# Linear attention in a fused attention and mixture-of-experts kernel: key-value sums with the features as weights, in two column halves

## The chip, the cores and the metric

One core of a Trainium2 chip runs the whole program. The metric is device time in microseconds (us), the median of several executions. TensorE (PE) multiplies, its weight loads are listed as PEld; VectorE (DVE), ScalarE (ACT) and GpSimd (POOL) do the rest, and SyncE (SP) issues most DMAs. Matrices are float32; the program issues one matmul instruction where the trace shows two.

## The reference

```python
def _attn_ref(q, k, v, w_phi):            # (4, 8, 576, 64) each
    def phi(x):
        proj = np.einsum('bhsd,df->bhsf', x, w_phi)              # f = 128
        proj = proj - np.max(np.abs(proj), axis=-1, keepdims=True)
        return np.concatenate([np.exp(proj), np.exp(-proj)], axis=-1)
    q_p, k_p = phi(q), phi(k)
    kv = np.einsum('bhsf,bhsd->bhfd', k_p, v)
    z = np.sum(k_p, axis=2)
    num = np.einsum('bhsf,bhfd->bhsd', q_p, kv)
    den = np.einsum('bhsf,bhf->bhs', q_p, z)[..., None] + 1e-06
    return num / den
```

The result, 2304 tokens of 512, goes through a first mixture of 8 experts (one expert per token, only for tokens whose product with `w_skip` is positive) and a second one in which every token passes every expert. The gate of the first needs, per token, its product with `w_gate` (8 columns) and `w_skip` (1 column): 9 columns more for each head.

## The kernel before

The attention comes first. Two batches and two heads make a unit; there are 8 units of 9 tiles of 128 rows each, for keys and for queries. The loop over `g` in `attention` has 37 passes, and this text counts them from 0. A pass projects two pairs of tiles (`pp`, line 130), centres them on DVE (`m` and `t`, lines 137 and 139, one after the other), takes both exponentials on ScalarE (`f`, lines 146 and 147), and meanwhile works on the features of the pass before: query features are turned on TensorE (`ptq`, line 200, copied to `fq`), key features go into the key-value sums (`kv`, line 160), and numerator, denominator and gate columns come out of `num` (`po`, line 210), which `finish` divides on DVE (`rd`, `x`, `lall`). TensorE, DVE and ScalarE run in the order in which the code is written; POOL's and SP's order is set by a scheduler.

In `kv_mm` the values are the weights (128 rows, 64 columns and a column of ones) and the 256 features stream. The sums stand in PSUM with the 65 value columns as partitions. When a batch of a unit is complete (16 times in all, called blocks here), ScalarE copies the sums out (`kvt`, line 172); in the next pass `augment` multiplies them by `aug`, a table with an identity and the head's gate columns, which turns them and appends 9 columns (`pa`, line 187), and ScalarE copies that to `kvf` (line 194). `pt`, `ptq`, `pa` and `po` share four PSUM banks in turn.

The finished rows go to DRAM three times for the first two batches (`xd0`, `xd`, `x2d`), and twice for the others. After the first half, `Router.route` computes each token's place, and nine scatters on POOL write token numbers into `idx`. From pass 26 on the generator `moe1` fetches the first expert's weights (`fetch`, `fetch2`), and from pass 28 it splits one eighth of them into high and low parts at the end of each pass (`w1h` on ScalarE, `w1l` on DVE). The first expert slot starts when the attention ends.

Of the kernel before, what the change touches and what calls it, by code (L numbers as in the profile page):

```python
# [7 lines left out]
F32 = mybir.dt.float32  # L8
# [4 lines left out]
AF = mybir.ActivationFunctionType  # L13
# [5 lines left out]
P = 128  # L19
B, H, S, DH, FH = 4, 8, 576, 64, 128  # L20
# [18 lines left out]
def attention(tc, nc, cp, q, k, v, w_phi, w_gate, w_skip, lgs, routed, stepped, early, last_steps):  # L39
# [3 lines left out]
    with ExitStack() as ctx:  # L43
        c1 = ctx.enter_context(tc.tile_pool(name="c1", bufs=1))
        wk = ctx.enter_context(tc.tile_pool(name="wk", bufs=2))
        ps = ctx.enter_context(tc.tile_pool(name="psA", bufs=1, space=PSUM))
# [8 lines left out]
            nc.vector.memset(tab, 0.0)  # L55
            nc.scalar.activation(tab, tab, AF.Exp)

        aug = c1.tile([65, H, P], F32, name="aug")

        def load_aug():  # L60
            nc.gpsimd.memset(aug, 0.0)
            nc.sync.dma_start(aug[0:64, :, 65:73], w_gate.rearrange("(h d) e -> d h e", d=DH))
            nc.sync.dma_start(aug[0:64, :, 73:74], w_skip.rearrange("(h d o) -> d h o", d=DH, o=1))
            nc.gpsimd.tensor_copy(aug[:, :, 0:65], ident[0:65, 0:65].unsqueeze(1).to_broadcast([65, H, 65]))

        lall = c1.tile([P, 672], F32, name="lall")[:, 0 : NJ * H * 9].rearrange("p (j h e) -> p j h e", j=NJ, h=H)

        def bank(shape, nm):
            return ps.tile(shape, F32, name=nm, tag="W", bufs=4)
# [80 lines left out]
        def kv_mm(f, i, w):  # L150
            u, j = divmod(w, NJ)
            vt = st["vt", u]
            bs = [b for b in range(2) if 4 * b <= j <= 4 + 4 * b]
            for b in bs:
                if j == 4 * b:
                    st["acc", b] = ps.tile([65, 2, 256], F32, name="kv", tag="K", bufs=2)
            for h in range(2):
                for b in bs:
                    pr = slice(0, P) if j != 4 else slice(64 * b, 64 * b + 64)
                    nc.tensor.matmul(  # L160
                        st["acc", b][:, h],
                        vt[pr, j, h, 0:65],
                        f[pr, i % 2, i // 2 * 2 + h].rearrange("p s f -> p (s f)"),
                        start=(j == 4 * b and h == 0),
                        stop=(j == 4 * b + 4 and h == 1),
                        skip_group_check=True,
                    )
            done = [(u, b) for b in bs if j == 4 * b + 4]
            for u, b in done:
                kvt = wk.tile([65, 2, 256], F32, name="kvt", tag="kvt")  # L170
                st["kvt", u, b] = kvt
                late.append(lambda kvt=kvt, acc=st["acc", b]: nc.scalar.activation(kvt, acc, AF.Copy))
            if j == NJ - 1:
                load("vt", u + 2)
            return done

        def augment(u, b):
            kvt = st.pop(("kvt", u, b))
            hp = units[u][1]
            if b == 0:  # L180
                st["kv", u] = wk.tile([P, 608], F32, name="kvf", tag="kvf")[:, 0:592].rearrange(
                    "p (b h s f) -> p b h s f", b=2, h=2, s=2
                )
            pa = bank([P, 2, 2, P], "pa")
            for h in range(2):
                for fb in range(2):
                    nc.tensor.matmul(
                        pa[:, h, fb],
                        kvt[:, h, fb * P : fb * P + P],
                        aug[:, 2 * hp + h],  # L190
                        start=True,
                        stop=True,
                    )
            nc.scalar.activation(st["kv", u][:, b], pa[:, :, :, 0:74], AF.Copy)

        def q_tr(f, i, fq, o):
            pt = bank([P, 4, P], "ptq")
# [59 lines left out]

        for nm, u in (("kt", 0), ("vt", 0), ("kt", 1), ("qt", 0)):
            load(nm, u)
        load_aug()  # L260
        for nm, u in (("vt", 1), ("qt", 1)):
            load(nm, u)
        for u in (2, 3):
# [10 lines left out]
        with tc.manual_schedule(engines={nc.tensor.engine, nc.vector.engine, nc.scalar.engine}):  # L274
            busy(9)
            th = transp(steps[0])
            busy(8)
            for g in range(len(steps) + 1):
                cur = steps[g] if g < len(steps) else []
                if cur:  # L280
                    if g:
                        t = center(proj(th))
                    else:
                        nth = transp(steps[1])
                        t = center(proj(th))
                        th = nth
                        busy(16)
                    if 0 < g < len(steps) - 1:
                        th = transp(steps[g + 1])
                    if g == 1:  # L290
                        busy(8)
                tl = {m: [(2 * i + r, w + r) for i, (nm, w) in enumerate(prev) if nm == m for r in range(2)] for m in "kq"}
                qs = tl["q"]
                fqs = []
                for o, (i, w) in enumerate(qs):
                    if o % 2 == 0:
                        fqs.append(wk.tile([P, 2, 4, P], F32, name="fq", tag="fq"))
                    q_tr(f, i, fqs[-1], o % 2)
                for ub in aug_todo:
                    augment(*ub)  # L300
                aug_todo = []
                f_ = expo(t) if cur else None
                for i, w in tl["k"]:
                    aug_todo += kv_mm(f, i, w)
                for c in late:
                    c()
                late.clear()
                if not cur:
                    last_steps(ps)
                for o, fq in enumerate(fqs):  # L310
                    ws_ = [w for _, w in qs[2 * o : 2 * o + 2]]
                    finish(ws_, num(ws_, fq))
                f, prev = f_, cur
                stepped()
                if cur:
                    early(g)
# [223 lines left out]
def moe1(tc, nc, c, rt, w1, w2, idx, xd, xd0, x2d, route, end):  # L540

    with ExitStack() as ctx:
# [7 lines left out]
        tabs = []  # L550
        xTs = [[early.tile([P, NKB, SLOT], F32R, name=nm) for nm in ("xTh0", "xTl0")]]

        def fetch(s):
            t, i = (first[s], 0) if s < 2 else (tabs[1], s - 2)
            e = nc.sync.value_load(t[0:1, 0, i : i + 1], min_val=0, max_val=E - 1)
            r = nc.sync.value_load(t[0:1, 1, i : i + 1], min_val=0, max_val=NIDX - SLOT)
            if s == 0:
                load_r1(e)
            src, n = (xd0, NTOK // 2) if s < 2 else (xd, NTOK)
            ix, xg = ixs[s % 3], xgs[s % 3]  # L560
            ins = nc.sync.dma_start(ix, idx[bass.ds(r, SLOT)].rearrange("(a p) o -> p a o", p=P))
            if s in (0, 2):
                for o in rt.scatters:
                    tc.add_manual_dep(
                        ins.ins,
                        o.ins.name,
                        mybir.DependencyInfo(mybir.DependencyClass.Sync, mybir.DependencyReason.DATA),
                        reason="the list is complete",
                    )
            nc.gpsimd.memset(xg, 0.0)  # L570
            for a in range(2):
                nc.gpsimd.indirect_dma_start(
                    out=xg[:, a],
                    out_offset=None,
                    in_=src[:, :],
                    in_offset=bass.IndirectOffsetOnAxis(ap=ix[:, a].bitcast(U32), axis=0),
                    bounds_check=n - 1,
                    oob_is_err=False,
                )
            if s:  # L580
                load_r1(e)
            return e

        def load_r1(e):
            for kb in range(NKB):
                nc.sync.dma_start(
                    r1[:, kb], w1[bass.ds(e, 1), kb * P : kb * P + P].rearrange("o p f -> p (o f)")
                )

        def fetch2(e):  # L590
            for f in range(0, NFB, 2):
                nc.sync.dma_start(
                    r2[:, f : f + 2],
                    w2[bass.ds(e, 1), f * P : f * P + 2 * P].rearrange("o (b p) d -> p (o b) d", p=P),
                )
# [5 lines left out]
        def split_w1(i):  # L601
            kb, h = divmod(i, 2)
            sl = slice(512 * h, 512 * h + 512)
            split_w(w1h[:, kb, sl], w1l[:, kb, sl], r1[:, kb, sl])
# [87 lines left out]
                    slot(s)  # L692
                    chain(s + 1)

        rt.scatter()
        es = rt.early_slots()
        first = [next(es)]
        fetch2(fetch(0))
        yield
        first.append(next(es))  # L700
        done, psA = 0, None
        while psA is None:
            psA = yield
            for i in range(done, min(8, done + 1) if psA is None else 8):
                split_w1(i)
                done += 1
        e1 = fetch(1)
# [452 lines left out]
def tile_kernel(  # L1160
# [25 lines left out]
    late, gates = [], []  # L1186

    def stepped():
        rt.scatter(3)
        if gates:  # L1190
            gates.pop(0)()

# [74 lines left out]
```

## Time and profile before

| | |
|---|---|
| median of 3 runs | 2007.0 us (2003.72 to 2011.33) |
| the profiled execution | 2020.51 us, of it 2018.7 us span |
| attention, from the start to the first matmul of the first slot | 239.8 us |
| TensorE busy over the span | 1982.6 us (98%) |
| mean granted clock over the span | 0.992 |

A busy TensorE isn't TensorE at its peak, since the ends of matmuls are modelled; so the text goes by the distance from one group's start to the next one's. DMA share is the mean busy share of 16 DMA engines; over 1 means that packets overlap, which is a full queue.

### The profile page before, as it was taken

The page shows a single profiled execution, that of the slowest core. Times are in us where ns is not written, and L with a number is a line of the kernel's source. Part 1 is how long each engine was busy: PE and PEld are TensorE (multiplying, and loading weights), DVE is VectorE, ACT ScalarE, POOL GpSimd, SP SyncE. Part 2 cuts the span into 40 slices and gives each one's busy share as a digit, 9 for nine tenths or more (in the row PEclk, how much of TensorE's full clock was granted, in tenths as well). Part 3 has the DMA queues.
Part 4 walks back from the last instruction along what each step waited for, and adds up shares of the span by engine and source line. Part 5 has one row for each costly group of instructions (what it writes and reads, how often), then busy time and mean ns, then how long its engine had stood idle before and what let it go on. Part 6 is the DMA issues. An engine that isn't in the chain of part 4 may idle for free.

```text
span 2018.7 us, 30705 instructions
## 1 busy us (share of the span) xinstructions
PE 1982.6 (98%) x11752; PEld 1748.9 (87%) x11752; DVE 1250.4 (62%) x2134; ACT 893.9 (44%) x1706; POOL 339.2 (17%) x281
## 2 busy tenths in 40 slices
PE   9999999989999999999999999999999999999999
PEld 7877899986788988989888999899988888898997
DVE  4555777765676666666646666665664666556663
ACT  5665745545443433434344343343434434334441
POOL 1002032211112121121012212112101121212210
PEclk9998999999999999999999999999999999999999
DMA  7996776645312122131121212213112121221211
GB/s 167 105 133 143 124 235 221 216 154 169 107 36 84 49 77 73 53 115 55 45 83 59 84 42 84 74 53 115 52 48 89 53 84 42 84 74 53 84 53 42
DMA packets 163355, 187.40 MB, mean 93 GB/s; under 512 B 38334, under 2 KB 116926, under 8 KB 163196
## 3 DMA queue, kind: packets, MB, share of 16 engines
q1 hardware_dynamic: 159580, 178.17, 32.1%
q0 software_dynamic: 3456, 7.09, 1.1%
q8 instruction: 95, 1.56, 0.3%
q14 instruction: 64, 0.52, 0.1%
q10 hardware_dynamic: 160, 0.07, 0.0%
HBM read 163.70 MB, written 23.96 MB: 93 GB/s over the span
## 4 chain that ended last, share of the span: by engine, by line
PE 71%; DMA 3%; DVE 2%; ACT 1%; SPq 1%; issue 0%; ACTq 0%
PE py L1016 36%; PE pb L980 14%; PE pd L980 9%; PE pa L980 9%; DMA r<-in_moe_w_dram 3%; PE pg L857 1%; PE warm L730 1%; SPq L777 1%; DVE wcl L807 1%; ACT w2h L966 0%; PE pt L849 0%; DVE hl L1001 0%; DMA xr<-x2d 0%; DVE c L1068 0%; ACT v L988 0%
## 5 line engine op out<-in xcount | busy, mean ns | idle before, releaser
L1016 PE MATMUL py<-w2l,hh 128*128 128x512 f32 x1152 | 452.3, 393 | 0.0
L1016 PE MATMUL py<-w2h,hh 128*128 128x512 f32 x1152 | 451.6, 392 | 0.0
L1016 PE MATMUL py<-w2h,hl 128*128 128x512 f32 x1152 | 451.1, 392 | 0.0
L971 DVE TENSOR_TENSOR w2l<-r,w2h 128x512 fp32r<-128x512 f32 x184 | 175.8, 962 | 209.2 <-ACT w2h L966 209.2
L1016 PEld LDWEIGHTS py<-w2l,hh 128*128 128x128 f32 x1152 | 216.5, 188 | 49.0 <-issue 0.6
L1016 PEld LDWEIGHTS py<-w2h,hl 128*128 128x128 f32 x1152 | 216.6, 188 | 37.6
L1016 PEld LDWEIGHTS py<-w2h,hh 128*128 128x128 f32 x1152 | 216.8, 188 | 36.1
L1027 DVE SCALAR_TENSOR_TENSOR acc<-py,lg,acc 128x512 f32<-128x512 f32 x264 | 196.9, 746 | 67.2 <-PE py L1016 66.4
L996 ACT ACTIVATE hh<-c 128x384 fp32r<-128x384 f32 x192 | 100.9, 525 | 215.6 <-DVE c L1056 119.8
L966 ACT ACTIVATE w2h<-r 128x512 fp32r<-128x512 f32 x184 | 114.7, 624 | 174.9 <-DMA r<-in_moe_w_dram 174.5
L809 POOL TENSOR_TENSOR r<-r,s 128x512 f32<-128x512 f32 x45 | 58.1, 1292 | 661.9 <-DVE wcl L807 650.5
L980 PE MATMUL pb<-xch,wch 128*128 128x384 f32 x576 | 150.2, 342 | 9.4 <-ACT v L988 6.6
L807 DVE TENSOR_TENSOR wcl<-r,wch 128x512 fp32r<-128x512 f32 x230 | 154.3, 686 | 7.1 <-DVEq L691 4.0
L789 POOL TENSOR_TENSOR s<-r 128x512 f32<-128x512 f32 x45 | 58.4, 1298 | 586.1 <-DMA r<-in_moe_w_dram 586.1
L980 PE MATMUL pb<-xcl,wch 128*128 128x384 f32 x576 | 147.9, 338 | 0.0
L980 PE MATMUL pb<-xch,wcl 128*128 128x384 f32 x576 | 147.4, 337 | 0.0
L801 ACT ACTIVATE wch<-r 128x512 fp32r<-128x512 f32 x230 | 138.7, 622 | 9.7 <-PE pd L980 3.0
L980 PEld LDWEIGHTS pb<-xch,wch 128*128 128x128 f32 x576 | 104.6, 188 | 31.5 <-ACT v L988 14.3
L1040 DVE TENSOR_TENSOR pb<-pb,s 128x384 f32<-128x384 f32 x96 | 54.3, 566 | 120.6 <-PE pb L980 65.7
L988 ACT ACTIVATE s<-pa 128x384 f32<-128x384 f32 x96 | 47.1, 491 | 173.5 <-PE pa L980 173.5
L1001 DVE SCALAR_TENSOR_TENSOR hl<-c,hh 128x384 fp32r<-128x384 f32 x192 | 106.6, 555 | 6.9 <-ACT hh L996 6.9
L988 ACT ACTIVATE z<-pb 128x384 f32<-128x384 f32 x96 | 47.1, 491 | 139.3 <-PE pb L980 139.3
(234 smaller groups left out, 3621.2 us busy)
## 6 DMA issues: line engine op xcount, KB each, us to landing
r<-in_moe_w_dram SPq DMA_DIRECT2D x168, 512.0 KB
r<-in_moe_w_dram SPq DMA_DIRECT2D x184, 256.0 KB
xd<-x SPq DMA_DIRECT2D x12, 576.0 KB
qt<-in_q_dram SPq DMA_DIRECT2D x16, 288.0 KB
x2d<-x SPq DMA_DIRECT2D x8, 576.0 KB
xr<-x2d SPq DMA_DIRECT2D x18, 256.0 KB
out_dram<-acc SPq DMA_DIRECT2D x18, 256.0 KB
kt<-in_k_dram SPq DMA_DIRECT2D x16, 256.0 KB
```

The source lines that it names most:

```text
L789: g.tensor_tensor(s1, a21, a22, ALU.add)
L801: nc.scalar.activation(wc[m, i][0], wsrc[m][i], AF.Copy)
L807: nc.vector.tensor_tensor(l, src[i], f32(h), ALU.subtract)
L809: (nc.gpsimd if m else nc.vector).tensor_tensor(src[3], src[2], src[6], ALU.subtract)
L966: nc.scalar.activation(h, w2r[m, b], AF.Copy)
L971: nc.vector.tensor_tensor(l, w2r.pop((m, b)), f32(h), ALU.subtract)
L980: nc.tensor.matmul(dst, w[:, kb, sl], x[:, kb], start=(start and m == 0), stop=(stop and m == 5), skip_group_check=True,)
L988: nc.scalar.activation(t, src, AF.Copy)
L996: nc.scalar.activation(hh, src, AF.Relu)
L1001: nc.vector.scalar_tensor_tensor(hl, src, 0.0, f32(hh), ALU.max, ALU.subtract)
L1016: nc.tensor.matmul(py, ht[:, i * P : i * P + P], wt, start=(m == 0), stop=(m == 11))
L1027: nc.vector.scalar_tensor_tensor(accs[t], py, lg[:, t, e : e + 1], accs[t], ALU.mult, ALU.add)
```

## The change

The key-value sums are made the other way round: 64 feature columns are the weights and the 65 value columns stream. Each 256-feature product becomes four, one for each sign (`fb`) and column half (`c`), and the two halves go to the two column halves of the array. The sums then stand with features as partitions, as `num` wants them. At the end of a block ScalarE copies them straight into `kvf`, DVE copies the 64 value columns of both heads into `k2`, and in the next pass `turn_kv` turns `k2` with two transposes for both heads, ScalarE copies the result, and `gate_kv` multiplies it by the gate table `wgd` (18 columns, both heads), which DVE copies into `kvf`. The table `aug` and its identity go.

Outside the attention: a pass issues one scatter instead of three, the call that issued all that were left at pass 26 goes, and `fetch` is split, so that the first slot's index list and gather (`fetch_x(0)`) come behind its weights, at the sixth split.

```diff
-                    st["acc", b] = ps.tile([65, 2, 256], F32, name="kv", tag="K", bufs=2)
+                    st["acc", b] = ps.tile([P, 2, 2, 65], F32, name="kv", tag="K", bufs=2)
             for h in range(2):
...
-                        vt[pr, j, h, 0:65],
-                        f[pr, i % 2, i // 2 * 2 + h].rearrange("p s f -> p (s f)"),
...
+                for fb in range(2):
+                    for b in bs:
+                        pr, r = (slice(0, P), 0) if j != 4 else (slice(64 * b, 64 * b + 64), 64 * b)
+                        for c in range(2):
+                            nc.tensor.matmul(
+                                st["acc", b][64 * c : 64 * c + 64, h, fb],
+                                f[pr, i % 2, i // 2 * 2 + h, fb, 64 * c : 64 * c + 64],
+                                vt[pr, j, h, 0:65],
...
+                                tile_position=(r, 64 * c),
...
-        def augment(u, b):
...
+            nc.scalar.activation(st["kv", u][:, b, :, :, 0:65], acc, AF.Copy)
+            k2 = st["k2", u, b] = wk.tile([P, 2, 2, DH], F32, name="k2", tag="k2")
+            nc.vector.tensor_copy(k2.rearrange("p s h d -> p h s d"), acc[:, :, :, 0:DH])
+
+        def turn_kv(u, b):
+            k2 = st.pop(("k2", u, b))
+            pt = bank([P, 2, P], "ptk")
+            for fb in range(2):
+                nc.tensor.transpose(pt[:, fb], k2[:, fb].rearrange("p h d -> p (h d)"), ident)
+            kvt = st["kvt", u, b] = wk.tile([P, 2, P], F32, name="kvt", tag="kvt")
+            nc.scalar.activation(kvt, pt, AF.Copy)
+
+        def gate_kv(u, b):
+            kvt = st.pop(("kvt", u, b))
+            pg = bank([P, 2, 2, 9], "pgk")
+            for fb in range(2):
+                nc.tensor.matmul(
+                    pg[:, fb].rearrange("p h e -> p (h e)"),
+                    kvt[:, fb],
+                    wgd[:, units[u][1]].rearrange("p h e -> p (h e)"),
...
+            nc.vector.tensor_copy(st["kv", u][:, b, :, :, 65:74].rearrange("p h s e -> p s h e"), pg)
...
+                for ub in aug_todo:
+                    turn_kv(*ub)
                 for o, (i, w) in enumerate(qs):
...
                 for ub in aug_todo:
-                    augment(*ub)
+                    gate_kv(*ub)
...
-        rt.scatter()
         es = rt.early_slots()
         first = [next(es)]
-        fetch2(fetch(0))
+        fetch2(fetch_w(0))
...
+                if i == 5:
+                    fetch_x(0)
                 split_w1(i)
...
-        rt.scatter(3)
+        rt.scatter(1)
```

On TensorE, a pass that also handles a finished block (a block pass), before and then after. `ptk` is the turned `k2`, `pgk` the gate columns.

```order
L130 MATMUL pp<-ws,th 128x128 x8
L113 MATMUL pt<-ident,kt 128x128 x2
L113 MATMUL pt<-ident,qt 128x128 x2
L200 MATMUL ptq<-ident,f 128x128 x8
L187 MATMUL pa<-aug,kvt 128x128 x4
L160 MATMUL kv<-f,vt 65x256 x4
L210 MATMUL po<-kvf,fq 64x74 x16
```

```order
L131 MATMUL pp<-ws,th 128x128 x8
L114 MATMUL pt<-ident,kt 128x128 x2
L114 MATMUL pt<-ident,qt 128x128 x2
L192 MATMUL ptk<-ident,k_709 128x128 x2
L213 MATMUL ptq<-ident,f 128x128 x8
L200 MATMUL pgk<-wgd,kvt 128x18 x2
L163 MATMUL kv<-vt,f 64x65 x16
L223 MATMUL po<-kvf,fq 64x74 x16
```

Four products of 256 columns have become sixteen of 65; the turn stands ahead of `ptq`, the gate product behind it.

On ScalarE, from the exponentials of the pass in which a block ends to those of the next, before and then after, with what each row waits for.

```order
L146 ACTIVATE f<-t 128x8x128 [waits DVE_49]
L147 ACTIVATE f<-t 128x8x128
L172 ACTIVATE kvt<-kv 65x512 [waits PE_49]
L117 ACTIVATE th<-pt 128x512 [waits PE_49,Activation_49]
L201 ACTIVATE fq<-ptq 128x512 [waits PE_49,Activation_49]
L201 ACTIVATE fq<-ptq 128x512 [waits PE_49]
L194 ACTIVATE kvf<-pa 128x296 [waits PE_49]
```

```order
L147 ACTIVATE f<-t 128x8x128 [waits DVE_49]
L148 ACTIVATE f<-t 128x8x128
L184 ACTIVATE kvf<-kv 128x4x65 [waits PE_49]
L118 ACTIVATE th<-pt 128x512 [waits PE_49,Activation_49]
L194 ACTIVATE kvt<-ptk 128x256 [waits PE_49]
L214 ACTIVATE fq<-ptq 128x512 [waits PE_49,Activation_49]
L214 ACTIVATE fq<-ptq 128x512 [waits PE_49]
```

The copy out of the sums still stands behind both exponentials; the second copy moved ahead of the two `fq`.

On DVE in the same stretch, before and then after (`k_709` is a `k2`).

```order
L137 TENSOR_REDUCE m<-pp 128x8 [waits PE_49]
L139 TENSOR_TENSOR t<-pp,m 128x1024 [waits DVE_49,Activation_49]
L224 TENSOR_SCALAR rd<-po 128x4 [waits PE_49]
L225 RECIPROCAL rd<-rd 128x4 [waits DVE_49]
L233 TENSOR_TENSOR x<-po,rd 128x2x2x64 [waits DVE_49]
L239 TENSOR_TENSOR lall<-po,rd 128x2x2x9
```

```order
L138 TENSOR_REDUCE m<-pp 128x8 [waits PE_49]
L140 TENSOR_TENSOR t<-pp,m 128x1024 [waits DVE_49,Activation_49]
L186 COPY k_709<-kv 128x2x2x64 [waits Activation_49]
L237 TENSOR_SCALAR rd<-po 128x4 [waits PE_49]
L238 RECIPROCAL rd<-rd 128x4 [waits DVE_49]
L246 TENSOR_TENSOR x<-po,rd 128x2x2x64 [waits DVE_49]
L252 TENSOR_TENSOR lall<-po,rd 128x2x2x9
```

A copy has come in ahead of the four instructions of `finish`, and it waits for ScalarE, whose `kvf<-kv` reads the same sums.

On POOL, the nine scatters of the first half up to the first gather, before and then after.

```order
L435 DMA idx<-ids,di 20480x1 [waits DVE_49]
L435 DMA idx<-ids,di 20480x1 x6
L84 MEMSET vt 128x18x2 [waits DMAHW2_49,DMAHW5_49,DMAHW1_49,DMAHW6_49,DMAHW0_49,DMAHW7_49,PE_49,Pool_49]
L435 DMA idx<-ids,di 20480x1
L435 DMA idx<-ids,di 20480x1 [waits DMASW0_49]
```

```order
L450 DMA idx<-ids,di 20480x1 [waits DVE_49]
L450 DMA idx<-ids,di 20480x1 x4
L85 MEMSET vt 128x18x2 [waits DMAHW2_49,DMAHW3_49,DMAHW1_49,DMAHW4_49,DMAHW0_49,DMAHW7_49,PE_49,Pool_49]
L450 DMA idx<-ids,di 20480x1 x3
L450 DMA idx<-ids,di 20480x1 [waits DMASW0_49]
```

The memset of a value tile has moved up by two scatters; between the scatters stands nothing else.

## Rows read from the trace of the kernel before

**Rows 1.** Start to first slot: stretch, length, busy PE, PEld, DVE, ACT, POOL, clock, DMA
```profile
0.00:239.80 239.80, 229.68 (x2675) 183.93 (x2675) 132.40 (x277) 148.98 (x228) 23.79 (x53) 0.97 0.80 136
```

**Rows 2.** TensorE's order of time, a block pass: start, us, group
```profile
121.48 1.16 PE L130 MATMUL pp<-ws,th 64*128 64x128 f32 x16
...
123.07 1.04 PE L200 MATMUL ptq<-ident,f 128*128 128x128 f32 x8
123.94 1.06 PE L187 MATMUL pa<-aug,kvt 65*128 65x128 f32 x8
124.83 1.89 PE L160 MATMUL kv<-f,vt 128*65 128x256 f32 x8
126.66 1.25 PE L210 MATMUL po<-kvf,fq 128*64 128x74 f32 x32
127.84 1.16 PE L130 MATMUL pp<-ws,th 64*128 64x128 f32 x16
```

**Rows 3.** TensorE's order of time, ends of a plain pass
```profile
41.13 1.16 PE L130 MATMUL pp<-ws,th 64*128 64x128 f32 x16
...
46.59 1.16 PE L130 MATMUL pp<-ws,th 64*128 64x128 f32 x16
```

**Rows 4.** Groups by line, start to 240 us: shapes, count, busy us, mean ns
```profile
L160 PE MATMUL kv<-f,vt 128*65 128x256 f32 (+1 forms) x320 | 72.3, 394 | 0.0
L210 PE MATMUL po<-kvf,fq 128*64 128x74 f32 x1152 | 45.5, 232 | 0.4 <-issue 0.4
```

**Rows 5.** DVE and ScalarE in order of time, the block pass of rows 2
```profile
121.60 0.16 DVE L224 TENSOR_SCALAR rd<-po 128x4 f32<-128x4 f32 x1 [2.11 <-PE po L210]
...
122.35 0.18 DVE L239 TENSOR_TENSOR lall<-po,rd 128x36 f32<-128x36 f32 x1
...
124.02 1.22 DVE L139 TENSOR_TENSOR t<-pp,m 128x1024 f32<-128x1024 f32 x1
...
125.03 0.42 ACT L194 ACTIVATE kvf<-pa 128x296 f32<-128x296 f32 x1
125.35 1.05 ACT L146 ACTIVATE f<-t 128x1024 f32<-128x1024 f32 x1
126.29 1.05 ACT L147 ACTIVATE f<-t 128x1024 f32<-128x1024 f32 x1
```

**Rows 6.** ScalarE's order of time from pass 29, with the weight splits
```profile
197.14 1.06 ACT L146 ACTIVATE f<-t 128x1024 f32<-128x1024 f32 x1 [1.76 <-DVE t L139]
...
199.52 0.62 ACT L598 ACTIVATE w1h<-r 128x512 fp32r<-128x512 f32 x1
...
203.35 1.06 ACT L146 ACTIVATE f<-t 128x1024 f32<-128x1024 f32 x1 [1.46 <-DVE t L139]
...
209.09 1.06 ACT L146 ACTIVATE f<-t 128x1024 f32<-128x1024 f32 x1 [1.70 <-DVE t L139]
```

**Rows 7.** TensorE's order of time around 103 us
```profile
99.80 1.16 PE L130 MATMUL pp<-ws,th 64*128 64x128 f32 x16
...
105.24 0.59 PE L187 MATMUL pa<-aug,kvt 65*128 65x128 f32 x3 [2.26 <-issue]
...
110.26 1.16 PE L130 MATMUL pp<-ws,th 64*128 64x128 f32 x16
```

**Rows 8.** DMA queues, start to 240 us: instruction packets, MB, share
```profile
q8 instruction: 21, 0.34, 0.7%
```

**Rows 9.** DMA queues, 84 to 102 us
```profile
q8 instruction: 1, 0.02, 0.4%
```

**Rows 10.** Busy time of each engine while one unit's rows are stored
```profile
87.00:101.00 14.00, 14.00 (x193) 11.68 (x190) 7.49 (x16) 9.58 (x15) 0.13 (x1) 1.00 1.26 83
```

**Rows 11.** TensorE's order of time, the pass that holds the scatters
```profile
159.14 1.18 PE L130 MATMUL pp<-ws,th 64*128 64x128 f32 x16
...
174.06 1.16 PE L130 MATMUL pp<-ws,th 64*128 64x128 f32 x16
```

**Rows 12.** SP's issues in order of time, the first index list
```profile
187.17 0.38 SPq L561 DMA_DIRECT2D ix<-idx  x1
```

More of the change, by code (lines that the diff above doesn't have):

```diff
@@ L56, in attention, with load_gates @@
             nc.scalar.activation(tab, tab, AF.Exp)
[L58 to L64, printed above, removed]
+        wgd = c1.tile([P, 96], F32, name="wgd")[:, 0:72].rearrange("p (a h e) -> p a h e", a=4, h=2)
+        def load_gates():
+            nc.gpsimd.memset(wgd, 0.0)
+            for h in range(2):
+                r = slice(64 * h, 64 * h + 64)
+                nc.sync.dma_start(wgd[r, :, h, 0:8], w_gate.rearrange("(a h d) e -> h d a e", h=2, d=DH)[h])
+                nc.sync.dma_start(wgd[r, :, h, 8:9], w_skip.rearrange("(a h d o) -> h d a o", h=2, d=DH, o=1)[h])
         lall = c1.tile([P, 672], F32, name="lall")[:, 0 : NJ * H * 9].rearrange("p (j h e) -> p j h e", j=NJ, h=H)
@@ L155, in kv_mm @@
                 if j == 4 * b:
-                    st["acc", b] = ps.tile([65, 2, 256], F32, name="kv", tag="K", bufs=2)
+                    st["acc", b] = ps.tile([P, 2, 2, 65], F32, name="kv", tag="K", bufs=2)
             for h in range(2):
[L158 to L161, printed above, removed]
-                        vt[pr, j, h, 0:65],
-                        f[pr, i % 2, i // 2 * 2 + h].rearrange("p s f -> p (s f)"),
[L164 to L167, printed above, removed]
+                for fb in range(2):
[6 more added lines that the diff above has]
+                                vt[pr, j, h, 0:65],
+                                start=(j == 4 * b and h == 0 and fb == 0),
+                                stop=(j == 4 * b + 4 and h == 1 and fb == 1),
+                                tile_position=(r, 64 * c),
+                                skip_group_check=True,
+                            )
             done = [(u, b) for b in bs if j == 4 * b + 4]
             for u, b in done:
-                kvt = wk.tile([65, 2, 256], F32, name="kvt", tag="kvt")
-                st["kvt", u, b] = kvt
-                late.append(lambda kvt=kvt, acc=st["acc", b]: nc.scalar.activation(kvt, acc, AF.Copy))
+                late.append(lambda u=u, b=b, acc=st["acc", b]: copied(u, b, acc))
             if j == NJ - 1:
@@ L175, in kv_mm, with copied @@
             return done
-        def augment(u, b):
-            kvt = st.pop(("kvt", u, b))
-            hp = units[u][1]
+        def copied(u, b, acc):
             if b == 0:
@@ L183, in augment @@
                 )
[L184 to L194, printed above, removed]
+            nc.scalar.activation(st["kv", u][:, b, :, :, 0:65], acc, AF.Copy)
[16 more added lines that the diff above has]
+                    wgd[:, units[u][1]].rearrange("p h e -> p (h e)"),
+                    start=True,
+                    stop=True,
+                )
+            nc.vector.tensor_copy(st["kv", u][:, b, :, :, 65:74].rearrange("p h s e -> p s h e"), pg)
         def q_tr(f, i, fq, o):
@@ L259, in attention @@
             load(nm, u)
-        load_aug()
+        load_gates()
         for nm, u in (("vt", 1), ("qt", 1)):
@@ L551, in moe1, with fetch_w, fetch_x @@
         xTs = [[early.tile([P, NKB, SLOT], F32R, name=nm) for nm in ("xTh0", "xTl0")]]
-        def fetch(s):
+        def fetch_w(s):
             t, i = (first[s], 0) if s < 2 else (tabs[1], s - 2)
             e = nc.sync.value_load(t[0:1, 0, i : i + 1], min_val=0, max_val=E - 1)
+            if s < 1:
+                load_r1(e)
+            return e
+        def fetch_x(s):
+            t, i = (first[s], 0) if s < 2 else (tabs[1], s - 2)
             r = nc.sync.value_load(t[0:1, 1, i : i + 1], min_val=0, max_val=NIDX - SLOT)
-            if s == 0:
-                load_r1(e)
             src, n = (xd0, NTOK // 2) if s < 2 else (xd, NTOK)
@@ L579, in fetch @@
                 )
-            if s:
-                load_r1(e)
+        def fetch(s):
+            e = fetch_w(s)
+            fetch_x(s)
+            load_r1(e)
             return e
```

## The prediction

> **What bounds the kernel now.** I read the busy times by stretch first. Up to the first matmul of the first expert slot, at 239.8 us, TensorE is busy 229.68 us, DVE 132.40 and ScalarE 148.98 [rows 1]. So TensorE sets the pace of the attention, and all that the change touches lies in it; behind it TensorE goes on without a break, so a shorter attention brings the end forward by as much. Then I read TensorE's order of time: from one `pp` to the next a block pass takes 6.36 us, one group's start right on the last [rows 2], and a plain pass 5.46 [rows 3]. Three things break this rhythm. From pass 28 on ScalarE's exponentials come every 6.21 us in a pass with a block and 5.74 in one without [rows 6]: there `t`, both `f`, `w1h`, `w1l`, `m` and the next `t` wait for one another in a ring, and TensorE follows it. At 103 us TensorE stands for 2.26 us on nothing that the program waits for, and the pass takes 10.46 us instead of 6.36 [rows 7]. And the pass that holds the scatters takes 14.92 us, 8.56 too many [rows 11].
>
> The profiled execution took 2020.5 us, the median of the runs is 2007.0. I make the sum as a difference on the profiled one and carry it over to the median; the 12.7 us of the two long passes may not be in every run, and I count on neither.
>
> **The change part by part.**
>
> *Key-value sums.* Now 320 matmul instructions take 72.3 us [rows 4], 1.83 us for 8 in a pass [rows 2]. Afterwards there are four times as many, 1280, of 64 weight columns and 65 streamed. The nearest row is `po`, which is already cut into column halves with 64 weight columns and 74 streamed: 32 of them from one start to the next group's take 1.18 us, 36.9 ns each [rows 2]. That makes 1280 x 36.9 = 47.2 us, a saving of 25.1, or 0.65 in a usual pass. Bounds: by `po`'s whole busy time 45.5 / 1152 = 39.5 ns [rows 4], 50.6 us and a saving of 21.7; if the price falls with the streamed columns, 65/74 of 36.9 is 32.4 ns, 41.5 us and a saving of 30.8. I take 25.1, as the weights are the same as `po`'s.
>
> The Trainium skill, TensorE: Matmul & The Clock Gate, section LDWEIGHTS, gives a weight load the time of its columns over 1.2 GHz, and the section on packing small matmuls says that loads overlap running matmuls only in other row groups. By that, an estimate from the page, 64 columns are 53 ns and 1280 loads 68 us, which leaves a saving of 4. The trace speaks against it: a `po`, load included, passes in 36.9 ns [rows 2], in the same row groups.
>
> *The block.* `pa` is 8 instructions in 0.89 us [rows 2]. In its place come two transposes and four instructions with 128 weight columns. Eight transposes of `ptq` pass in 0.87 [rows 2], 0.11 each; a gate instruction at `pa`'s 0.11 makes 0.44. So 0.66 instead of 0.89, 0.23 less.
>
> *The wait that comes with it.* DVE's copy `k2` stands ahead of `finish` and waits for ScalarE's copy of the same sums, which stands behind both exponentials. In rows of the block pass: `t` ends 3.76 us after `pp` starts, the two `f` end 5.86 after it [rows 2, 5]. A copy of 0.42 [rows 5] each on ScalarE and then DVE brings `k2` to 6.7. TensorE comes to the turn one plain pass later, 5.46 - 0.65 = 4.81, plus the 1.59 from `pp` to `ptq` [rows 2]: 6.4. It waits 0.3, and some 0.1 for the signal. Queued behind the copy on DVE are the four instructions of `finish`, 0.93 long [rows 5], so `po`'s bank comes free at 7.7; `po`, `pt`, `ptk` and `ptq` are four banks, so the second `ptq` needs it, and TensorE is there at 6.8 + 0.22 + 0.44 = 7.5. Together some 0.65 a block. It may be 0.3, if the copies are short, or 1.1, if signals are slow. The gate columns' own copies cost nothing: queries run some six passes behind keys, so `num` needs them later.
>
> *Where the saving isn't paid out.* In the ring from pass 28 TensorE's time doesn't count. Of the sums' 320 instructions 52 lie there, 16%, so 21.0 of the 25.1 remain. Twelve of the 16 blocks lie ahead: their work saves 12 x 0.23 = 2.8, their waits cost 12 x 0.65 = 7.8 (3.6 to 13.2). The other four sit in the ring itself: `finish` used to be done before ScalarE's `w1h` ended, now copy and `finish`, 0.42 + 0.93, follow ScalarE's copy, while `w1h` needs 0.62 [rows 6] there: 0.7 longer each, 3 together.
>
> TensorE's path: -21.0 - 2.8 + 7.8 + 3 = **-13 us** (-22 to -4).
>
> *Instructions.* 21 packets of 16 KB brought TensorE's 2 x 2675 loads and matmuls up to 239.8 us [rows 1, 8], 255 a packet. While one unit's rows are stored the DMA share is 1.26, and TensorE uses 383 instructions in 14 us [rows 10], a packet every 9.3. In the 18 us up to 102 only one came [rows 9], and the stop at 103 followed; it cost 10.46 - 6.36 = 4.1 us [rows 2, 7]. So a packet waits behind stores. After the change a plain pass has 184 instructions instead of 136, in 4.81 us instead of 5.46: 38 a us against 25. The same delay is ridden out less often. There are eight stretches of stores, one for each unit. Bounds: no further stop, 0; a stop in each of them, 7 x 4.1 = 29. I take two more, **+8**, as before only the worst delay told, and a reserve shorter by a third lets the next ones through.
>
> The Trainium skill, Runtime: NRT & Kernel Launch, section Instruction fetch mechanics, says the same of the size (16 KiB blocks, 256 instructions) and that crossing a block is mostly hidden. The trace agrees on the size, and at 103 us it wasn't hidden. By the page the sum would be -13.
>
> *Scatters and fetch.* POOL's order still has the nine scatters in a row, so I expect the long pass of rows 11 as it is: 0. If fewer at once did help, up to 8.6 would go; that is the other bound. The first index list was issued at 187.17 [rows 12], 13 us after that pass had ended, so SP did not stand there; moving it behind the weight loads costs nothing, and the first slot needs the gather only at 239.8. The loads of the gate table replace those of `aug` in the same place of SP's queue, two issues more.
>
> Sum: -13 + 8 = **-5**, so 2015 for an execution like the profiled one and **2002** for the median.
>
> **The rivals.** *Instructions keep up* (the saving is paid out): the stop at 103 stays the only one, as two delays of such a length are rare. For it, it was one in 21 packets; against it, the rate. -13, so 1994.
>
> *The burst goes too*: the memset moved up, or other timing, spares the 8.6 us. For it, the long pass coincides with the scatters; against it, their order. -13.6, so 1993, or less without stops.
>
> *TensorE starves* (slower): in each stretch of stores a packet comes late. -13 + 29 = +16, so 2023. It decides from the fifth further stop on: five cost 20.5, more than the path's 13 and most of 10. For it, all eight stretches look like that of rows 10; against it, TensorE now waits for `k2` anyway and needs fewer instructions then.
>
> *The weight loads don't overlap*, by the page's rule above: the 1280 take 68 us, the sums save 4 instead of 25 before the ring's share, and the path comes out at +5: 2012. Against it stands `po`.
>
> **How the numbers follow.** About 0.5%, 10 us, is what a measurement of this kernel can tell from no change. My forecast, within 10 us of the old time, has 0.45, instructions keep up 0.25, the burst goes 0.12, TensorE starves 0.13, slow loads 0.05. So faster 0.37, same 0.50, slower 0.13. The range reaches from 1984, a path at its lower bound with no further stop, to 2020, three quarters of the starving case.
>
> **What would show it.** Right: `kv` as 1280 instructions in some 47 us; plain passes of 4.8 us and block passes of 6.1; a wait of TensorE at the turn for DVE's copy, 12 times some 0.4; exponentials every 5.7 and 6.9 us from pass 28; two or three more stops on `issue` of over 2 us while stores run, and the scatters' pass as long as before. Wrong: block passes of 5.5, which would mean that the copy is in time; ScalarE waiting for the first expert's weights at the first split, since the stores ahead of them in the queue don't get faster; or no stops at all.

## The result, and the profile after

| | before | changed kernel |
|---|---|---|
| median | 2008.4 us (7 runs, 2003.7 to 2013.4) | 2019.3 us (7 runs, 2012.8 to 2024.4) |
| ratio, 95% interval | | 1.0051 (1.0030 to 1.0072) |
| traced execution, its span | 2020.5, 2018.7 | 2012.8, 2011.1 |
| start to the first slot | 239.8 us | 237.5 us |
| TensorE busy up to 240 us | 229.9 us | 206.1 us |

The changed kernel is slower by some 10 us; 2002 was forecast. The two traced executions must not be set against each other by their spans: the one of before lies 12 us above its median, the other 6 below. What can be compared is stretches.

TensorE works 24 us less in the attention, and yet the attention ends only 2.3 us earlier. Even that is too kind to the change: the traced execution of before holds the 8.6 us of [rows 11], and before_again below, which doesn't, ends its attention at 234.0 us, 3.4 us ahead of the changed kernel. The groups by line, from the start to 240 us (shape, count, busy us, mean ns, then idle time ahead of them and its cause):

```profile
L223 PE MATMUL po<-kvf,fq 128*64 128x74 f32 x1152 | 48.5, 239 | 7.1 <-issue 6.2 <-ACT fq L214 0.9
L163 PE MATMUL kv<-vt,f 128*64 128x65 f32 (+1 forms) x1280 | 43.8, 226 | 9.5 <-issue 9.5
```

Against [rows 4] the sums fell from 72.3 to 43.8 us, and the idle time on `issue` ahead of the two, 0.4 us then, is now 15.7 (the one stop of before, [rows 7], stood ahead of `pa`). TensorE's waits of the same stretch (line, waited for: us, times, longest) put it in order:

```profile
PE kv L163 <- issue: 9.5, 3, 7.2
PE po L223 <- issue: 6.2, 3, 4.1
PE pp L131 <- DVE t L140: 5.3, 7, 1.8
PE ptk L192 <- DVE k L186: 5.0, 6, 1.0
PE ptq L213 <- ACT f L148: 1.6, 5, 0.6
```

The first two are most of the loss. The third is mostly the ring from pass 28 (4.0 of the 5.3 us), the fourth the new wait for `k2`.

Where nothing stops it, the loop runs as hoped and better. TensorE's order of time in a plain pass and at the start of the next, which has a block (start, us, group):

```profile
36.21 1.16 PE L131 MATMUL pp<-ws,th 64*128 64x128 f32 x16
...
38.76 1.15 PE L163 MATMUL kv<-vt,f 128*64 128x65 f32 x32
39.74 1.21 PE L223 MATMUL po<-kvf,fq 128*64 128x74 f32 x32
40.88 1.16 PE L131 MATMUL pp<-ws,th 64*128 64x128 f32 x16
...
42.80 0.44 PE L192 MATMUL ptk<-ident,k 128*128 128x128 f32 x2 [0.17 <-DVE k L186]
...
44.19 0.52 PE L200 MATMUL pgk<-wgd,kvt 128*128 128x18 f32 x4
44.64 1.15 PE L163 MATMUL kv<-vt,f 128*64 128x65 f32 x32
```

From one `pp` to the next 4.67 us in place of 5.46 [rows 3]; the 32 instructions of `kv` pass in 39.74 - 38.76 = 0.98 us, 30.6 ns each, where before 8 took 1.83 [rows 2].

The longest stop, in pass 15:

```profile
90.54 1.16 PE L131 MATMUL pp<-ws,th 64*128 64x128 f32 x16
...
93.09 0.74 PE L163 MATMUL kv<-vt,f 128*64 128x65 f32 x17
101.04 1.02 PE L163 MATMUL kv<-vt,f 128*64 128x65 f32 x14 [7.21 <-issue]
...
101.96 2.11 PE L223 MATMUL po<-kvf,fq 128*64 128x74 f32 x31
104.00 1.16 PE L131 MATMUL pp<-ws,th 64*128 64x128 f32 x16
```

The pass takes 13.46 us in place of 4.67: 7.21 of standing, and behind it about half the clock (`po` from 101.96 to 104.00, 2.04 us at a mean granted clock of 0.53, against 1.14 us in the pass above). The instruction packets of that time (queue: packets, MB, share), from 98 to 100 us:

```profile
q8 instruction: 1, 0.02, 3.2%
```

It is the only one that starts between 82 and 100 us. Busy times of the stretches that wait for a packet in this way, each with a store of three copies in it (stretch, length, then busy us and instructions of PE, PEld, DVE, ACT, POOL, clock, DMA share, GB/s):

```profile
53.00:68.00 15.00, 12.91 (x249) 11.41 (x248) 9.05 (x16) 10.95 (x17) 0.13 (x1) 1.00 1.16 112
82.00:99.00 17.00, 11.77 (x229) 10.41 (x227) 8.61 (x16) 11.22 (x17) 0.00 (x0) 0.94 1.20 120
116.00:128.00 12.00, 11.94 (x238) 10.65 (x238) 6.60 (x15) 8.09 (x13) 0.00 (x0) 1.00 1.19 103
```

In each TensorE uses 456 to 497 instructions, loads and matmuls together, and then has none. In the kernel before the same happens once: its last packet before the stop landed at 85.8 us and the next one started at 102.7, 17 us later [rows 7, 9, 10].

The count from the start says it more exactly. In this trace, and below in after_again and sums_alone, TensorE stands in passes 11, 15 and 20 after its 1100th, 1480th and 1984th matmul, when 7, 10 and 14 packets had landed. The kernel before stands after its 1094th, with 7 packets, in both of its traces; full_cols, below, after its 845th and 1223rd, with 5 and 8. Each time the loads and matmuls used (two for one matmul) are 102 to 128 short of 256 for every packet landed and for two more. So, as an estimate from these counts, TensorE has two packets' worth in hand at the start, never gets further ahead than that, and stands when they are used up; the 102 to 128 would be its other instructions, which the counts leave out. Each of these stops ends 1.2 to 1.8 us after a packet has landed. The 1.89 us in pass 25 are not of this kind: 19 packets had landed, 398 instructions were left by the same count, and the last packet was 5.7 us old. What TensorE waited for there stays open.

For the rest of the text I count over **passes 10 to 21**, from the first `pp` of pass 10 to that of pass 22: the stores of three units land in it, and neither the scatters nor the ring. The row of this stretch before, and then of the changed kernel:

```profile
64.17:139.67 75.50, 73.24 (x877) 58.87 (x873) 39.91 (x74) 47.68 (x73) 0.40 (x3) 0.98 1.02 134
56.26:139.78 83.52, 69.05 (x1177) 62.62 (x1173) 42.56 (x86) 47.88 (x74) 0.40 (x3) 0.90 0.92 124
```

The changed kernel comes to pass 10 7.9 us earlier, and has nothing left of it at pass 22.

### The profile page after: what moved, and what is told of

It is laid out like the page before. It is cut to its first block, busy times and chain, and to the rows that moved or that the text cites. A ratio compares the mean times of both kernels' runs of the same rounds, so it can differ in the third digit from the quotient of the medians.

```text
span 2011.1 us, 32593 instructions
## 1 busy us (share of the span) xinstructions
PE 1952.2 (97%) x12680; PEld 1743.9 (87%) x12680; DVE 1253.9 (62%) x2166; ACT 893.1 (44%) x1706; POOL 337.3 (17%) x280
## 4 chain that ended last, share of the span: by engine, by line
PE 72%; DMA 2%; DVE 2%; ACT 1%; SPq 0%; issue 0%; ACTq 0%; DVEq 0%
PE py L1039 37%; PE pb L1003 14%; PE pd L1003 9%; PE pa L1003 9%; DMA r<-in_moe_w_dram 2%; PE pg L880 1%; PE warm L753 1%; SPq L800 0%; DVE wcl L830 0%; DMA xr<-x2d 0%; ACT w2h L989 0%; PE pt L872 0%; ACT xch L936 0%; DVE w2l L994 0%; DVE hl L1024 0%
```

## The experiments

**Theory A**: TensorE's instructions arrive in packets that stand behind the stores of rows; TensorE has some 500, two packets' worth, in reserve; the new sums use them up faster, so it stops in each stretch of stores. **Theory B**: the scatters and the divided fetch cost the time. Open besides was what the wait for `k2` costs. A table of all runs stands at the end of this section.

**Both kernels once more.** No edit.

> The changed kernel once more, for a second execution with a trace and a better ratio. Theory A (TensorE's instructions come late while rows are stored): again three to five stops on `issue` of over 1.8 us between 59 and 190 us, each ending right after a 16 KB instruction packet has come, though not in the same passes; plain passes of 4.67 us elsewhere; 2012 to 2024. Theory B (the other part, scatters and fetch, costs the time): the stops are chance, and the loss against the kernel before lies behind 150 us.

> The kernel before once more, for a second execution with its trace: how much of its 12.7 us in two long passes is in every execution. Theory A (late instructions while rows are stored): the stop near 103 us is there again, 4 to 6 us, since its cause is, and the 8.6 us at the scatters aren't; span some 2010. If both are there, they belong to the kernel; if neither, the loss of the changed kernel is larger than its stops alone.

The changed kernel: 2027.6 us against 2015.4 on the same chip, ratio 1.0052 (1.0032 to 1.0071); before against itself 1.0012 (1.0000 to 1.0025). The changed kernel's stops are there again, 4.0, 8.6 and 2.7 us, and not in other passes, as I had expected, but in 11, 15 and 20 once more and at the same instructions. A fourth of 3.1 us comes in pass 24, where the first trace just got by; it fits the count (4727 used with 17 packets, 137 short of 19 x 256). A stop of 1.4 us in pass 10 doesn't fit it. Passes 10 to 21 take 87.5 us. The kernel before has its one stop again, at 105.5 us, and 77.3 us:

```profile
101.99 0.72 PE L187 MATMUL pa<-aug,kvt 65*128 65x128 f32 x5
105.54 0.80 PE L187 MATMUL pa<-aug,kvt 65*128 65x128 f32 x3 [2.83 <-issue]
106.13 3.62 PE L160 MATMUL kv<-f,vt 128*65 128x256 f32 x8
```

The 8.6 us at the scatters aren't there this time. So the stops belong to the kernels, and the burst of [rows 11] comes and goes.

**One part at a time.** The new sums with the old scatters and fetch, and the other way round:

```diff
--- the changed kernel
+++ sums_alone
-        rt.scatter(1)
+        rt.scatter(3)
...
+        rt.scatter()
         es = rt.early_slots()
...
-        fetch2(fetch_w(0))
+        fetch2(fetch(0))
...
-                if i == 5:
-                    fetch_x(0)
```

> The changed kernel with the old scatters (three a pass and all the rest at pass 26) and the old undivided fetch, so the new sums and gate columns alone. A: the loss is in the sums, 2012 to 2024 as with both. B: without the other part the saving of the sums is paid out, 1994 to 2000.

> The kernel before with one scatter a pass and the divided fetch, its sums as they were. A: 2003 to 2013, no difference. B: 2015 or more.

1.0074 (1.0047 to 1.0101) for the sums alone, 1.0008 (0.9989 to 1.0026) for the moves alone. Their passes 10 to 21 take 86.7 and 76.1 us. B falls: the loss is in the sums.

**The same pass, more instructions.** The weights of `kv` in 128 columns:

```diff
--- the changed kernel
+++ full_cols
-                        for c in range(2):
-                            nc.tensor.matmul(
-                                st["acc", b][64 * c : 64 * c + 64, h, fb],
-                                f[pr, i % 2, i // 2 * 2 + h, fb, 64 * c : 64 * c + 64],
+                        nc.tensor.matmul(
+                            st["acc", b][:, h, fb],
+                            f[pr, i % 2, i // 2 * 2 + h, fb],
```

> The changed kernel with 128 feature columns as weights in place of two halves of 64: 640 instructions for the sums in place of 1280, a plain pass of 152 TensorE instructions in place of 184. A: if one takes 54 ns (65 columns at the 0.83 ns that a column takes in the 128-column turns, load hidden), the plain pass stays under 4.8 us, the reserve lasts a fifth longer, two stops at most are left, 1995 to 2008. If the load of 128 columns isn't hidden, some 107 ns each, plain passes of 5.2 us and 2005 to 2012. B: the stops don't count, and it stays at 2015 to 2022.

1.0108 (1.0075 to 1.0140), worse than either. A load of 128 columns isn't hidden; 16 instructions take 1.83 us, 114 ns each:

```profile
44.16 1.90 PE L162 MATMUL kv<-vt,f 128*128 128x65 f32 x16
45.99 1.26 PE L222 MATMUL po<-kvf,fq 128*64 128x74 f32 x32
```

So my numbers for its plain pass (under 4.8, or 5.2) were both too low; it is 5.47 us, as long as that of the kernel before, but of 152 instructions and not 136. That makes it another test of A, and a sharper one: 12% more instructions in the same time, and passes 10 to 21 take 87.2 us in place of 75.5, with two passes of 12.59 and 14.34 us where before had one of 10.46.

```profile
64.78:151.97 87.19, 77.87 (x969) 72.94 (x965) 42.23 (x86) 46.36 (x72) 0.39 (x3) 0.90 0.89 114
```

**A third of the stores.** The first two batches' rows go to `xd0` alone, and two DMAs in DRAM, issued on ScalarE, make the other copies:

```diff
--- the changed kernel (and before, in before_one_store)
+++ one_store
+    def copies():
+        h = NTOK // 2
+        nc.scalar.dma_start(xd[0:h, 0:D], xd0[0:h, 0:D])
+        nc.scalar.dma_start(x2d[0:h], xd0[0:h, 0:D])
...
+            if bp == 0 and i:
+                continue
```

> The changed kernel, with the first two batches' rows stored once in place of three times; the other two copies are made from the first in DRAM, behind its last store, in two DMAs. Up to 150 us a third of the stores are left. Theory A: the stops of TensorE in passes 10 to 12, 15, 16, 20 and 21, together 25 us over the usual passes, go; the copies cost up to 8 us later; faster than the kernel before by 5 to 15 us, a ratio of 0.992 to 0.998. Rival (the stops come from the number of instructions alone, or from the loads): the stops stay within 5 us of what they were, ratio 1.003 to 1.007.

> The kernel before with the same single store and copies. A: only the stop near 103 us is there to go, 5 us; less what the copies cost: ratio 0.996 to 1.002. With one_store this tells what the new sums bring when no store stands in the instructions' way: by A 8 to 15 us between the two.

The stops go, all but 2.18 us in pass 20: passes 10 to 21 take 67.7 us and not 83.5 to 87.5. The totals don't come out as forecast, 1.0010 (0.9993 to 1.0026) and 1.0056 (1.0037 to 1.0075), since the copies cost time elsewhere. The changed kernel saves 16 to 20 us in these passes and only some 8 in all, so that they cost it 7 to 12 us; the kernel before saves 3 to 5 us there (72.8 and not 75.5 to 77.3) and loses 9 to 11 in all, so that they cost it 12 to 16, where I had allowed up to 8. ScalarE issues them in the middle of the attention, and stands there until the last store has landed (ScalarE in order of time):

```profile
127.61 1.08 ACT L214 ACTIVATE fq<-ptq 128x512 f32<-128x512 f32 x2
132.56 0.54 ACTq L1211 DMA_DIRECT2D xd<-xd  x1
133.14 0.79 ACTq L1212 DMA_DIRECT2D x2d<-xd  x1
133.98 1.06 ACT L147 ACTIVATE f<-t 128x1024 f32<-128x1024 f32 x1 [5.30 <-issue]
```

That pass takes 13.04 us, and with the copies on the queues another takes 9.76. The two ratios, 1.0010 / 1.0056 or some 9 us, would tell what the new sums bring when fewer stores are in the way, if the copies cost both kernels alike; by the numbers above they don't.

**The same stores in longer runs.** Two units' rows lie side by side and go out together, 1 KB at a time:

```diff
--- the changed kernel (and before, in before_wide)
+++ wide_stores
-                if j == 0:
-                    st["x"] = c1.tile([P, NJ, P], F32, name="x", tag="x", bufs=3)
+                if j == 0 and hp % 2 == 0:
+                    st["x2"] = c1.tile([P, NJ, 2 * P], F32, name="x", tag="x", bufs=2)
+                if j == 0:
+                    st["x"] = st["x2"][:, :, hp % 2 * P : hp % 2 * P + P]
...
-                    routed(bp, x, hp, lg, lambda: bank([P, 512], "pr"))
+                    if hp % 2:
+                        routed(bp, st["x2"], hp, lg, lambda: bank([P, 512], "pr"))
...
-        sl = slice(hp * P, hp * P + P)
+        sl = slice(hp * P - P, hp * P + P)
```

> The changed kernel with rows of two units kept side by side and stored together: runs of 1 KB in place of 512 B, half as many packets, in half as many stretches. A: if a packet of 1 KB takes hardly longer than one of 512 B, half the stops' time goes, 10 to 15 us, ratio 0.998 to 1.001; if it takes twice as long, each stretch is twice as long and the stops are no shorter, ratio 1.003 to 1.008. Rival: no change, 1.005.

> The changed kernel with the wide stores once more, beside the next two on one chip: 0.993 to 0.997, no pass between 55 and 120 us more than 1.5 us over its usual time.

> The kernel before with the rows of two units stored together, in runs of 1 KB. Theory A: only its one stop near 103 us is there to go, 4 to 7 us: ratio 0.9965 to 0.998. Against the changed kernel with the same stores (0.9949) this gives what the new sums bring when instructions keep up: by A 4 to 8 us. Rival (the wide stores help for another reason than the instructions): both kernels gain alike from them, 20 us, ratio 0.990.

With the changed kernel 0.9949 (0.9931 to 0.9968) and, on another chip, 0.9936 (0.9915 to 0.9957): it is now faster than before by 10 to 13 us, with not one instruction of TensorE changed. The kernel before gains nothing that can be measured, 0.9989 (0.9973 to 1.0005), though its stop is gone too. Passes 10 to 21 in wide_again, and then in before_wide:

```profile
56.30:120.38 64.08, 62.54 (x1175) 56.21 (x1172) 41.96 (x86) 47.01 (x73) 0.40 (x3) 1.00 0.60 141
63.82:135.21 71.39, 71.39 (x876) 58.09 (x873) 39.93 (x74) 47.68 (x73) 0.40 (x3) 1.00 0.55 126
```

Full clock, and the same matmuls as in the changed kernel in 64.1 us and not 83.5. The stretch doesn't hold the same stores, though: in wide_again one store of two units, issued from 73.6 us, lies in it, and the next follows at 121.4, while the changed kernel has the stores of three units in it. So part of the fall of the DMA share, from 0.92 to 0.60, is fewer bytes. Packets of that stretch, changed kernel first (the queue that carries the stores, then the instructions), then wide_again:

```profile
q1 hardware_dynamic: 19660, 10.18, 91.4%
q8 instruction: 9, 0.15, 0.8%
```

```profile
q1 hardware_dynamic: 13520, 8.85, 58.7%
q8 instruction: 10, 0.16, 1.1%
```

Passes 10 to 27 hold the stores of the first four units in every kernel; they take 122.3 and 127.5 us in the changed kernel, 108.9 in wide_again and 103.2 in wide_stores, so the gain stands. While wide_again stores, the DMA share is over 1 too (the last number but one):

```profile
76.00:90.00 14.00, 13.22 (x271) 11.90 (x262) 8.00 (x19) 10.10 (x15) 0.13 (x1) 1.00 1.10 219
```

What differs is the speed. By the packets of the traces, one of 512 B took 74 to 89 ns (the means of the changed kernel's four stores), one of 1 KB 76 ns in wide_again's second store. So two units' rows (3.54 MB) go out in 16 us there, and one unit's (1.77 MB) took 14 to 18 us: half as many such stretches, each of about the same length. It is a narrow escape: in wide_again's first two stores the next instruction packet lands when TensorE is 39 and 4 instructions short of the place where after_again stands in passes 15 and 24, and wide_k2 below does stand at the second place, for 1.98 us.

My expectation for the changed kernel was too careful (half the stops' time; nearly all went), and the rival, that both kernels gain alike, falls.

**The rest, without the stops in the way.** wide_sums is sums_alone with the wide stores. In wide_k2 the two copies change places:

```diff
--- wide_stores
+++ wide_k2
-            nc.scalar.activation(st["kv", u][:, b, :, :, 0:65], acc, AF.Copy)
             k2 = st["k2", u, b] = wk.tile([P, 2, 2, DH], F32, name="k2", tag="k2")
             nc.vector.tensor_copy(k2.rearrange("p s h d -> p h s d"), acc[:, :, :, 0:DH])
+            nc.scalar.activation(st["kv", u][:, b, :, :, 0:65], acc, AF.Copy)
```

> The wide stores and the new sums with the old scatters and undivided fetch. If the other part of the change matters, it shows here, where no stop hides it: by the two earlier ratios of the changed kernel with and without it, 1.0052 and 1.0074, it may be worth 4 us; by theory A, which gives it no role, within 3 us of wide_again.

> The same with the wide stores, and DVE's copy `k2` issued ahead of ScalarE's copy of the same sums, so that it waits for TensorE alone and ScalarE's waits for it. If the wait for `k2` is on the path (TensorE waited 6.3 us for it in 9 turns, and from pass 28 `finish` stands behind it in the ring), 3 to 7 us less than wide_again, the passes with a block from pass 29 at 6.1 in place of 6.57. If ScalarE's later copy then holds up `th`, it comes out even.

wide_sums 0.9938 (0.9914 to 0.9963), as wide_again: the scatters and the fetch change nothing here either that can be measured. wide_k2 **0.9896** (0.9876 to 0.9915), 1999.6 us against 2020.2, the fastest of all and 8 us ahead of wide_again on the same chip, a little more than I had expected. A block pass:

```profile
40.57 1.16 PE L131 MATMUL pp<-ws,th 64*128 64x128 f32 x16
...
42.15 0.38 PE L192 MATMUL ptk<-ident,k 128*128 128x128 f32 x2
42.37 1.04 PE L213 MATMUL ptq<-ident,f 128*128 128x128 f32 x8
...
46.01 1.16 PE L131 MATMUL pp<-ws,th 64*128 64x128 f32 x16
```

5.44 us against 5.88 at the same place in the changed kernel, with no wait ahead of `ptk`. Passes 28 to 34 (the ring), in the kernel before, the changed one and wide_k2:

```profile
185.28:228.36 43.08, 42.97 (x547) 35.22 (x544) 29.79 (x68) 32.51 (x53) 5.02 (x5) 1.00 0.80 197
178.57:225.10 46.53, 38.44 (x692) 34.06 (x693) 30.89 (x76) 32.25 (x52) 5.02 (x5) 1.00 0.75 183
159.23:201.54 42.31, 38.63 (x692) 34.32 (x692) 30.93 (x76) 31.63 (x53) 5.00 (x5) 1.00 0.70 217
```

| kernel | ratio to before | passes 10 to 21 | clock there |
|---|---|---|---|
| before, twice | 1, 1.0012 | 75.5, 77.3 us | 0.98, 0.96 |
| moves_alone | 1.0008 | 76.1 | 0.98 |
| before_wide | 0.9989 | 71.4 | 1.00 |
| before_one_store | 1.0056 | 72.8 | 1.00 |
| changed, twice | 1.0051, 1.0052 | 83.5, 87.5 | 0.90, 0.88 |
| sums_alone | 1.0074 | 86.7 | 0.88 |
| full_cols | 1.0108 | 87.2 | 0.90 |
| one_store | 1.0010 | 67.7 | 0.97 |
| wide_stores, wide_again | 0.9949, 0.9936 | 64.6, 64.1 | 1.00, 1.00 |
| wide_sums | 0.9938 | 63.5 | 1.00 |
| wide_k2 | 0.9896 | 62.4 | 1.00 |

## Why the prediction was wrong, step by step

**What failed is the step on instructions: +8 where it was about +20.** From the medians: the wide stores take 1.0052 to 0.994, about 22 us, from the changed kernel, and 0.0011, about 2 us, from the one before. So the stops cost some 20 us more than they did. The rows of passes 10 to 21 say much the same, 83.52 - 64.08 = 19.4 (and 87.54 - 64.08 = 23.5 in the second trace) against 75.50 - 71.39 = 4.1, though fewer stores lie in that stretch with the wide ones. Of the 19.4 us TensorE stood 13.5 (0.4 and 4.1, 7.2, 1.9 in passes 11, 15 and 20); the rest, some 6, goes with the lower clock behind the stops, 0.90 over the stretch.

The mechanism stood in the text, and TensorE starving was a rival with 0.13 at 2023; it was this that came. The mistake was to let "a reserve shorter by a third lets the next ones through" stand for a number and then to take two stops of the old length. Both numbers were to be had: at the rate of [rows 10], 27 instructions a us, the 17 us between two packets around [rows 9] use up some 460, and then TensorE stood [rows 7]. That is the reserve. At the 38 a us that the text itself worked out, it lasts 12 us, so a wait of 17 gives a stop of 5; and four stretches with three copies lie in the first half. Four stops of 5, less the 4.1 that the kernel before already lost, are +16, and with the clock behind them more; against the path's -13 that was enough to forecast slower. Measured are 4.1, 7.2 and 1.9 us of standing in passes 11, 15 and 20 of the first trace, and 4.0, 8.6, 2.7 and 3.1 in passes 11, 15, 20 and 24 of the second: the stretches are alike in kind, not in length.

On this place the text weighed the Trainium skill, Runtime: NRT & Kernel Launch, section Instruction fetch mechanics, by which the crossing of a 16 KiB block is mostly hidden. The traces disagree: 7.21 us at one block here, 8.59 in after_again.

**Key-value sums: right in kind, too small.** 1280 instructions came, at 30.6 ns in place of 36.9: 39.2 us, a saving of 33.1 where the text had 25.1 and 30.8 at most. The bound that let the price fall with the streamed columns, 32.4, was the nearer one. The rival of slow loads drew on the Trainium skill, TensorE: Matmul & The Clock Gate, section on packing small matmuls; for column halves it falls, but for 128 columns full_cols shows a price of its kind, 114 ns with 65 columns streamed.

**Block work and the wait for `k2`: near.** The turn takes 0.22 and the gate product 0.45 us, as written. Blocks cost 1.05 to 1.21 us over a plain pass (5.72 and 5.88 against 4.67), where the text made 1.31. At the turn of pass 7 TensorE was some 0.3 us late (1.92 us from `pp` to `ptk`, 1.58 in wide_k2), where the text had 0.4, and wide_k2 shows the price of the place of the copy, 8 us by the ratios; the text had 7.8 and 3.

**The ring: right.** 46.53 - 43.08 = 3.5 us against 3. As wide_k2 gets to 42.31, it was indeed the copy ahead of `finish`.

**The path: -13 forecast, about -10 measured.** That is the wide stores with the new sums against the wide stores with the old ones, 0.9936 / 0.9989 on the same chip. By the traces of wide_again and before_wide: 7.5 us up to pass 10, 71.39 - 64.08 = 7.3 in passes 10 to 21 and 1.0 in passes 22 to 27, less 5.1 in the ring (one long pass of 9.81 us in it) and 0.9 behind it, 9.8. It lies within the -22 to -4 of the text. Of the larger saving of the sums not all arrived: passes 22 and 23, in which DVE also works on the routing, take 6.08 and 7.43 us, as they did (6.10 and 7.25). What became of the rest I haven't traced.

**Scatters and fetch: right, 0.** moves_alone and wide_sums show it. The burst of 8.6 us comes with neither kernel: it was in the first trace of before, in before_wide (a pass of 15.81 us) and, as passes of 11.20, 12.47 and 11.41 us, in wide_again, wide_sums and wide_k2, but not in before_again and wide_stores. What makes it stays open.

So -10 + 20 = +10, as measured; the two add up by construction, since both come from the same ratios, but the traces give each of them on its own. The range of 1984 to 2020 held the time by less than 1 us, which was luck; the sign was wrong.

## What to carry to other kernels

Before cutting one instruction into four, count instructions per microsecond and find the longest time in which no instruction packet comes; the product is to be held against what the engine used up before its one stop. The stop that came once in a trace was a threshold just reached here, and not a rare accident: it came at the same instruction in the next trace. Where small stores are in the way, longer runs of bytes may be worth more than the change itself: here they turned +10 us into -10 to -13. And a copy that waits for another engine's copy of the same data should be issued first by the engine that is free first.

## What the hardware showed that I had not expected

TensorE stood when the instruction packets that had landed and two more were used up, at the same instruction in every trace of a kernel: after 1100, 1480 and 1984 matmuls with 7, 10 and 14 packets in the changed kernel, after 1094 with 7 in the one before. The price of an instruction hangs on how its weights lie: 64 columns in alternating column halves 30.6 ns with 65 columns streamed, 128 columns 114 ns with the same 65, and 112 ns with 18 (`pgk`, 0.45 us for 4). A store's packet of 1 KB took 76 ns, one of 512 B 74 to 89, so that twice the bytes went out in the same 16 us.
